# Column-group steps in a work list: the tiling switch counted in a step's length instead of in its earliest begin

## The chip, the cores and the metric

The kernel runs on one core of a Trainium2 chip. The core has a matrix engine (TensorE, in the profile PE, and PEld for its weight loads), a vector engine (VectorE, DVE), a scalar engine (ScalarE, ACT), a gather and scatter engine (GpSimd, POOL) and a queue engine that issues most transfers (SyncE, SP). Each engine works through its own instructions in the order in which the program lists them; semaphores make one wait for another. The metric is device time of one execution in microseconds, lower is better.

## The reference

Three layers follow one another on 2 x 768 tokens of 512 numbers: an attention with a window of 128 and four sink keys, a mixture of four attention experts, and a feed-forward mixture of eight experts in which each token goes to one expert. Only the third is touched here:

```python
def _moe2_ref(x, w_gate, w_local, w1, w2):        # w1 (8, 512, 1024), w2 (8, 1024, 512)
    ...
            p = np.exp(ls); p /= p.sum() + 1e-09
            h = np.maximum(x[b, s] @ w1[e], 0.0)
            out[b, s] = p[e] * (h @ w2[e])
```

The expert `e` of a token is found on the chip from `x @ w_gate` and a gate `x @ w_local`.

## The kernel before

The feed-forward layer (FFN) sorts the tokens by expert into **units** of 128 token rows. A unit gathers its rows (`unit_front`, `ga`, on POOL), transposes them (`tr`, line 1442), multiplies them with the expert's `w1` in two halves of 512 columns (`unit_first`, destination `hp`), applies ReLU (line 1502), transposes the result and multiplies it with `w2` (`unit_second`, destination `yp`), and scatters the rows to the output (`unit_end`, line 1540). A product of fp32 numbers is made of three matmuls of split operands (`mm3`, lines 306 to 308), so each weight tile of 256 x 512 is first split in two: `sp` copies it to the high part on ACT (line 1413) and subtracts on DVE (line 1421). A unit has eight such tiles (`raw` 83 to 90 in this build). `ld` loads them from HBM by SP (line 1397); a unit whose expert is that of the unit before it has its eight loads skipped on the chip by a condition, so that they are issued but move nothing. A unit is 24 matmuls of 512 columns for the first layer (six for each weight tile) and 24 for the second.

Experts with few tokens left over don't get a unit. Up to four such remainders of at most 32 rows (`PC` = 4, `PSZ` = 32) are computed together in `pieces()`: TensorE is switched to column groups of 32, and the four remainders stand side by side, each with its own expert's weights in plain fp32. This is cut in 16 **steps** (numbered 0 to 15, `s_` in the code): steps 0 to 3 and 4 to 7 are the two halves of the first layer, 8 to 15 the second layer. A step is a matmul for each of the four groups (line 1640; plain fp32 makes two passes of each, so the profile has eight instructions a step) and needs four weight tiles of 128 x 512, 256 KB each, which SP loads into a ring `qw` of 3 x 4 - 1 = 11 tiles (lines 1628 and 1630). From step 3 on a load is skipped on the chip where its group is empty. After steps 3 and 7 ACT applies ReLU (line 1646), TensorE transposes (line 1610) and ACT copies (line 1612); the last step's result goes through ACT (line 1651) to a scatter on POOL (line 1654).

The order of all this is set by a work list, not by hand. Each piece of work is a `Task` with an engine, an estimated length, the tasks it needs, ring slots it takes and frees, and a priority. `Order.run` keeps for each engine the time at which it becomes free by the estimates, asks `ready` for the earliest begin of each piece that can go, and gives out the one with the earliest begin; of equal ones the one with the lower priority number. The parts that matter:

```python
    def ready(self, t):
        e = self.free.get(t.eng, 0.0)
        if t.eng == "PE" and t.rows != self.rows:
            e += self.TURN                  # 0.093
        ...
                e, t = min(c, key=lambda x: (x[0], x[1].prio))
        ...
            if t.eng == "PE":
                self.rows = t.rows
```

`rows` marks work in another tiling of TensorE. Before the change a step has `rows=True`, the units' work has not. The steps' priority numbers are 200 and up by one hundred for each four steps, a unit's are about one hundred times its number. SP's loads are tasks of the same list, so where a step goes decides where its loads stand in SP's queue.

Static code reaches to unit 10; then each engine reads a register and branches (lines 1708 and 1718) on whether there is a further unit. With the given inputs there are twelve units, 0 to 11: 0 to 5 of one expert, 6 of a second, 7 to 11 of a third; three of the four groups of the steps hold rows.

Of the kernel before, what the change touches and what calls it, by code (L numbers as in the profile page):

```python
# [186 lines left out]
def d_a(n, extra=0):  # L187
    return (n / 1.2 + 52 + 93 * extra) / 1000
# [11 lines left out]
def fused_kernel(  # L200
# [858 lines left out]
    def at2(b, i, e=0.0):  # L1059
        return int(G * (b * NT + i + LAG + b * LAG1 + ESP * e / E1))  # L1060
# [181 lines left out]
    prev = None  # L1242
# [27 lines left out]
    for j0, n in groups:  # L1270
# [3 lines left out]
        prev = route(j0, n, at2(j1 // NT, j1 % NT, E1) + (RPO if j1 < T - 1 else 10), prev)  # L1274
# [161 lines left out]
    fo = order  # L1436
# [156 lines left out]
    def pieces():  # L1593

        at = 100 * QU
        def regs():
            R["np"] = nc.sync.value_load(eui[0:1, 2:3], min_val=0, max_val=PC)
            for p_ in range(PC):
                R["eq", p_] = nc.sync.value_load(eui[32 + p_:33 + p_, 0:1], min_val=0, max_val=E2 - 1)

        def ga():
            nc.gpsimd.indirect_dma_start(out=R["xg", "q"], out_offset=None, in_=x2d,
                                         in_offset=bass.IndirectOffsetOnAxis(ap=gixq, axis=0))
        g = fo.add("POOL", 1.4, ga, deps=[K["gixq"], K["ga", 1], K["eui"]], acq=[("xg", ("xg", "q"))], prio=at - 60)
        g = fo.add("GD", 0.8, lambda: None, deps=[g], prio=at - 60)

        def turned(key, src, dst, deps, pr, rel=()):
            def pe():
                for j in range(4):
                    nc.tensor.transpose(R[key][:, j * 128:(j + 1) * 128], src()[:, j * 128:(j + 1) * 128], ident)  # L1610
            a = fo.add("PE", 4 * D_TR, pe, deps=deps, acq=[("B", key)], prio=pr, rel=rel)
            return fo.add("ACT", d_a(512), lambda: nc.scalar.activation(dst, R[key], AF.Copy), deps=[a], prio=pr, rel=[key])
        ready = turned(("pq", "x"), lambda: R["xg", "q"], xq, [g, K["pu"]], at - 30, [("xg", "q")])
        prev = None
        for s_ in range(16):
            n, d = divmod(s_, 4)
            pr = at + 100 * (s_ // QN) + 16

            def wl(s_, p_, n=n, d=d):
                def f():  # L1620
                    if s_ == 0 and p_ == 0:
                        regs()
                    e = bass.ds(R["eq", p_], 1)
                    src = w1[e, d * 128:(d + 1) * 128, n * 512:(n + 1) * 512] if n < 2 else \
                        w2[e, (n - 2) * 512 + d * 128:(n - 2) * 512 + (d + 1) * 128, :]
                    src = src.rearrange("e p f -> p (e f)")
                    if s_ < 3:
                        nc.sync.dma_start(R["qw", s_, p_], src)
                    else:
                        nc.sync.dma_start(R["qw", s_, p_], src, cond=R["np"] > p_)  # L1630
                return f
            lds = [fo.add("DMA", 0.73, wl(s_, p_), deps=[K["eui"]], acq=[("qw", ("qw", s_, p_))], prio=at - 100 + 25 * s_ + p_)
                   for p_ in range(PC)]
            bank = ("hq", min(n, 2))

            def mm(s_=s_, n=n, d=d, bank=bank):
                src = xq if n < 2 else hTq[n - 2]
                for p_ in range(PC):
                    rows = slice(PSZ * p_, PSZ * (p_ + 1))
                    nc.tensor.matmul(R[bank][rows, :], src[:, d * 128 + PSZ * p_:d * 128 + PSZ * (p_ + 1)], R["qw", s_, p_],  # L1640
                                     start=s_ in (0, 4, 8), stop=s_ in (3, 7, 15))
            need = ready if n < 2 else K["hTq", n - 2]
            prev = fo.add("PE", 0.9, mm, deps=lds + [need] + ([prev] if prev else []), rows=True,
                          acq=[("B", bank)] if s_ in (0, 4, 8) else [], rel=[("qw", s_, p_) for p_ in range(PC)], prio=pr)
            if s_ in (3, 7):
                r_ = fo.add("ACT", d_a(512), lambda bank=bank: nc.scalar.activation(hq, R[bank], AF.Relu),
                            deps=[prev] + ([K["hTq", 0]] if n else []), rel=[bank], prio=pr + 1)
                K["hTq", n] = turned(("pq", n), lambda: hq, hTq[n], [r_], pr + 1)

        def ev():  # L1650
            nc.scalar.activation(R["yo", "q"], R["hq", 2], AF.Copy, scale=puq)

        def sc_():
            sct = nc.gpsimd.indirect_dma_start(out=out_rows, out_offset=bass.IndirectOffsetOnAxis(ap=sixq, axis=0),
                                               in_=R["yo", "q"], in_offset=None, bounds_check=T * C - 1, oob_is_err=False)
            for x in last_sc:
                tc.declare_no_dep(sct.ins, x.ins, reason="units hold disjoint rows")
            last_sc.append(sct)
        e_ = fo.add("ACT", d_a(512), ev, deps=[prev, K["puq"]], acq=[("yo", ("yo", "q"))], rel=[("hq", 2)], prio=pr + 10)
        f_ = fo.add("POOL", 1.1, sc_, deps=[e_], prio=pr + 10)  # L1660
        fo.add("GD", 0.0, lambda: None, deps=[f_], rel=[("yo", "q")], prio=pr + 10)
# [31 lines left out]
    for u in range(TS):  # L1693
        if u == 0:
            continue
        unit_front(u)
        if u == 1:
            sp(0, 3, 1, 10)
            unit_second(0, (1,))
            probabilities()  # L1700
            unit_end(0)
            pieces()
        unit_first(u)
        if u > 1:
            unit_second(u - 1)
# [58 lines left out]
```

## Time and profile before

| | |
|---|---|
| median of three runs | 453.91 us (452.2 to 455.86) |
| the profiled execution | 454.28 us, of which the traced span is 452.6 us |
| TensorE busy | 430.1 us, 95% of the span |
| VectorE busy | 351.9 us, 78% |
| ScalarE busy | 322.9 us, 71% |
| GpSimd busy | 146.4 us, 32% |

TensorE's busy time counts a matmul from its start to a modelled end, and a matmul that waits inside for its operand counts as busy, so stretches are better judged by the distance between starts. The FFN takes the span from about 255 us on.

### The profile page before, as it was taken

The numbers are of one execution on the slowest core, as the hardware profiler recorded it, in microseconds if no ns is written. First come the engines' busy times: TensorE is split into PE (matmuls) and PEld (weight loads), VectorE is DVE, ScalarE is ACT, GpSimd is POOL, SyncE is SP. The second block draws the span as 40 slices with busy tenths as digits, with TensorE's granted clock in tenths as the row PEclk, the third lists the DMA queues.
The fourth block names the chain that finished last, engine by engine and source line by source line (L and its number), as shares of the span: only waits on it lengthen the run. The fifth ranks groups of instructions, "written<-read, shape, count | busy, mean of one in ns | idle before, by whom it ended". The sixth has DMA issues, their size and how long they took to land.

```text
span 452.6 us, 10520 instructions
## 1 busy us (share of the span) xinstructions
PE 430.1 (95%) x3486; PEld 332.2 (73%) x3486; DVE 351.9 (78%) x1019; ACT 322.9 (71%) x759; POOL 146.4 (32%) x214
## 2 busy tenths in 40 slices
PE   8899999999999999999988999999999999968894
PEld 4579988779889778978866767678888888822283
DVE  2999696986997799698699879899998999810090
ACT  4799685966976898587387428899998989710180
POOL 8189912354030024200691142504671200000011
PEclk9999999999999999999999999999999999989999
DMA  7987241300300000000650228660697110069401
GB/s 163 175 182 189 66 101 46 71 25 18 79 25 1 25 3 25 25 3 25 224 174 25 70 84 274 203 216 18 210 375 275 45 48 23 25 199 299 153 29 52
DMA packets 58590, 48.28 MB, mean 107 GB/s; under 512 B 40863, under 2 KB 42399, under 8 KB 58528
## 3 DMA queue, kind: packets, MB, share of 16 engines
q1 hardware_dynamic: 56368, 40.72, 30.8%
q0 software_dynamic: 2160, 6.82, 4.3%
q8 instruction: 29, 0.48, 0.4%
q14 instruction: 33, 0.27, 0.2%
HBM read 86.58 MB, written 6.55 MB: 206 GB/s over the span
## 4 chain that ended last, share of the span: by engine, by line
PE 46%; issue 23%; DVE 17%; ACT 7%; DMA 3%; POOL 2%; POOLq 0%; SPq 0%; another core or an unknown queue 0%; ACTq 0%; DVEq 0%
PE bank L673 7%; PE bank L306 7%; PE bank L721 7%; PE bank L308 6%; PE bank L307 6%; PE bank L401 4%; DVE P L687 3%; DVE pT L728 3%; DMA raw<-in_moe_w_dram 2%; ACT P L697 2%; DVE wqk_l L1421 2%; PE bank L738 2%; PE bank L736 2%; POOL out_dram L1540 2%; PE bank L737 2%
## 5 line engine op out<-in xcount | busy, mean ns | idle before, releaser
L697 ACT ACTIVATE P<-P,nm 128x260 f32<-128x260 f32 (+4 forms) x160 | 84.0, 529 | 18.7 <-DVE nm L687 17.0
L1421 DVE TENSOR_TENSOR w<-raw,w 128x1024 fp32r<-128x1024 f32 x44 | 52.4, 1222 | 36.7 <-ACT w L1413 36.7
L728 DVE TENSOR_TENSOR pT<-bank,pT 128x512 f16<-128x512 f32 (+1 forms) x96 | 58.1, 629 | 13.3 <-ACT pT L724 12.8
L1540 POOL DMA_INDIRECT out_dram<-yof,six x12 | 31.8, 2653 | 68.0 <-ACT yof L1537 66.7
L724 ACT ACTIVATE pT<-bank 128x512 f16<-128x512 f32 (+1 forms) x96 | 49.1, 550 | 6.0 <-PE bank L721 4.9
L721 PE MATMUL bank<-ident,P 128*128 128x128 f32 x344 | 50.3, 278 | 0.9 <-ACT P L697 0.6
L1413 ACT ACTIVATE w<-raw 128x1024 fp32r<-128x1024 f32 x44 | 45.3, 1061 | 8.2 <-DMA x2d<-x 5.3
L687 DVE CUSTOM_DVE_ANT_0 P<-bank,mask 128x260 f32<-128x260 f32 (+1 forms) x96 | 36.5, 405 | 8.6 <-PE bank L673 8.5
L721 PEld LDWEIGHTS bank<-ident,P 128*128 128x128 f32 x344 | 38.2, 142 | 4.7 <-ACT P L697 2.6
L736 PEld LDWEIGHTS <-pT 128*128 128x128 f16 x344 | 30.8, 98 | 8.7 <-issue 2.6
L738 PEld LDWEIGHTS <-pT 128*128 128x128 f16 x344 | 30.6, 98 | 4.1 <-DVE pT L728 3.8
L673 PE MATMUL bank<-kT,qT 64*128 64x260 f32 (+1 forms) x192 | 31.6, 414 | 1.5 <-issue 1.1
L737 PEld LDWEIGHTS <-pT 128*128 128x128 f16 x344 | 31.0, 98 | 1.0 <-issue 0.3
L697 ACT ACTIVATION_READ_ACCUMULATOR P<-P,nm 128x1 f32 x160 | 31.2, 195 | 0.0
L401 PE MATMUL bank<-ident,raw 128*128 128x128 f32 x168 | 28.7, 292 | 0.5 <-POOL mask L331 0.2
L306 PE MATMUL bank<-xT,wqk_h 128*128 128x256 f32 x96 | 28.8, 299 | 0.0
L636 POOL TENSOR_SCALAR raw<-raw,s_sv 128x256 f32<-128x256 f32 x20 | 18.7, 945 | 28.1 <-DVE si_sv L532 17.6
L308 PE MATMUL bank<-xT,wqk_l 128*128 128x256 f32 x96 | 27.1, 282 | 0.0
L307 PE MATMUL bank<-xT,wqk_h 128*128 128x256 f32 x96 | 27.0, 281 | 0.0
L401 PEld LDWEIGHTS bank<-ident,raw 128*128 128x128 f32 x168 | 20.6, 164 | 7.8 <-DVE nm L687 1.7
L639 POOL CAST v<-raw 128x512 f16<-128x512 f32 x10 | 6.1, 610 | 59.4 <-PE bank L738 34.7
L687 DVE CUSTOM_DVE_ANT_0 P<-bank,cmask 128x384 f32<-128x384 f32 (+3 forms) x48 | 24.4, 528 | 1.0 <-PE bank L673 0.8
(432 smaller groups left out, 1332.4 us busy)
## 6 DMA issues: line engine op xcount, KB each, us to landing
raw<-in_moe_w_dram SPq DMA_DIRECT2D x104, 512.0 KB
qw<-in_moe_w_dram SPq DMA_DIRECT2D x64, 256.0 KB
raw<-in_v_dram SPq DMA_DIRECT2D x12, 256.0 KB
x2d<-x SPq DMA_DIRECT2D x12, 256.0 KB
raw<-in_q_dram SPq DMA_DIRECT2D x11, 256.0 KB
raw<-in_k_dram SPq DMA_DIRECT2D x11, 256.0 KB
raw<-in_moe_wv_dram SPq DMA_DIRECT2D x1, 512.0 KB
raw<-in_moe_wq_dram SPq DMA_DIRECT2D x1, 512.0 KB
```

What stands on the lines that cost most here:

```text
L306: nc.tensor.matmul(o, l[0], r[0], start=start, stop=False)
L307: nc.tensor.matmul(o, l[0], r[1], start=False, stop=False)
L308: nc.tensor.matmul(o, l[1], r[0], start=False, stop=stop)
L401: nc.tensor.transpose(p[:, j * 128:(j + 1) * 128], src(j), ident)
L673: nc.tensor.matmul(o, l, r, start=True, stop=True)
L687: nc.vector.tensor_tensor_reduce(p, s, sg["mask"], 0.0 if dead and st == 1 else -scale, gr["nm"] if si else 3.0e38, op0=OP.add, op1=OP.min ...
L697: nc.scalar.activation(p, p, AF.Exp, bias=gr["nm"], scale=-1.0, accum_out=sg["sum"]())
L721: nc.tensor.transpose(R[tk][:, j * 128:(j + 1) * 128], R[gr["P"]][:, c:c + 128], ident)
L724: nc.scalar.activation(R[sk_][0][:, :n * 128], R[tk][:, :n * 128], AF.Copy)
L728: nc.vector.tensor_sub(pl[:, :n * 128], R[tk][:, :n * 128], ph[:, :n * 128])
L1413: nc.scalar.activation(R["w", u, c, hf][0], R["raw", u, c, hf], AF.Copy)
L1421: eng.tensor_sub(wl[:, :, s_], R["raw", u, c, hf][:, :, s_], f32(wh)[:, :, s_])
```

## The change

The steps lose the mark `rows=True`, so `ready` adds nothing to the begin of a step, or to that of the piece behind it, and their length in the work list goes from 0.9 to 1.0.

```diff
@@ -1640,7 +1640,7 @@
             need = ready if n < 2 else K["hTq", n - 2]
-            prev = fo.add("PE", 0.9, mm, deps=lds + [need] + ([prev] if prev else []), rows=True,
+            prev = fo.add("PE", 1.0, mm, deps=lds + [need] + ([prev] if prev else []),
                           acq=[("B", bank)] if s_ in (0, 4, 8) else [], rel=[("qw", s_, p_) for p_ in range(PC)], prio=pr)
```

The matmuls are the same; their order isn't. The listings give an engine's instructions in a row, the line, the operation, what it writes and what it reads. `qw` are the steps' weight tiles, `ux` the transposed rows of a unit, `hT` those of its hidden layer, `wo`, `w_0`, `w_1`, `xT`, `wqk`, `wvg` slots that hold split weights.

On TensorE, in the first layer of unit 2, before the change:

```order
L307 MATMUL bank_80<-wo_l,ux_0_350 128x512
L308 MATMUL bank_80<-wo_h,ux_1_351 128x512
L306 MATMUL bank_80<-w_0_4402,ux_0_350 128x512
L307 MATMUL bank_80<-w_1_4403,ux_0_350 128x512
L308 MATMUL bank_80<-w_0_4402,ux_1_351 128x512
```

and after it, at the same place:

```order
L308 MATMUL bank_80<-wo_h,ux_1_351 128x512
L1442 MATMUL bank_82<-ident,hs_0_348 128x128 x4
L1640 MATMUL bank_77<-qw_0_4392,v2h_208 32x512
L1640 MATMUL bank_77<-qw_0_4393,v2h_208 32x512
L1640 MATMUL bank_77<-qw_0_4394,v2h_208 32x512
L1640 MATMUL bank_77<-qw_0_4395,v2h_208 32x512
L1640 MATMUL bank_76<-qw_0_4396,v2h_208 32x512
L1640 MATMUL bank_76<-qw_0_4397,v2h_208 32x512
L1640 MATMUL bank_76<-qw_0_4398,v2h_208 32x512
L1640 MATMUL bank_76<-qw_0_4391,v2h_208 32x512
L1610 MATMUL bank_79<-ident,v2l_209 128x128 x4
L306 MATMUL bank_80<-w_0_4402,ux_0_350 128x512
```

Steps 3 and 4 now stand between the third and the fourth weight tile of unit 2. In the whole listing steps 0 and 1 have moved ahead of the last twelve matmuls of unit 0, step 2 behind these, 5 to 7 ahead of and into unit 2's second layer, 8 to 10 around unit 3's second layer, 11 to 13 behind unit 4's first layer, 14 and 15 behind unit 5's; that makes twelve places. Before the change steps 0 and 1 and steps 2 and 3 were two places, and 4 to 15 a third.

On TensorE, at the end of the static code, before the change:

```order
L308 MATMUL bank_76<-wqk_h,hT_1_355 128x512
L1442 MATMUL bank_77<-ident,xgf_0_4412 128x128 x4
L1640 MATMUL bank_82<-qw_0_4396,v2h_208 32x512
L1640 MATMUL bank_82<-qw_0_4397,v2h_208 32x512
L1640 MATMUL bank_82<-qw_0_4398,v2h_208 32x512
```

and after it:

```order
L307 MATMUL bank_78<-w_1_4409,hT_0_354 128x512
L308 MATMUL bank_78<-w_0_4408,hT_1_355 128x512
L1442 MATMUL bank_82<-ident,xgf_0_4412 128x128 x4
L1708 TENSOR_LOAD eui
L1718 COMPARE_AND_BRANCH
```

The 48 matmuls of the twelve steps 4 to 15 that stood between the transposes of unit 11 and the branch are gone from there, with one set of four transposes among them.

On SP, whose loads the steps' waits reach, behind the third of unit 2's eight weight tiles, before the change:

```order
L1397 DMA raw_0_85<-in_moe_w_dram 128x2x512
L1397 ISA
L1397 REGISTER_ALU
L1397 ISA
L1397 DMA raw_0_86<-in_moe_w_dram 128x2x512
```

and after it, ahead of the fourth:

```order
L1630 ISA
L1630 DMA qw_0_4398<-in_moe_w_dram 128x512
L1630 ISA
L1630 DMA qw_0_4391<-in_moe_w_dram 128x512
L1397 ISA
L1397 REGISTER_ALU
L1397 ISA
L1397 DMA raw_0_86<-in_moe_w_dram 128x2x512
```

Nine loads of steps 2 to 4 now stand between the third and the fourth tile of unit 2; the last of them, into tile 4391, can be issued only when step 2 has read what is in it. In the same way loads of steps 5 to 8 stand ahead of unit 3's tiles and among them, 9 to 13 among those of units 3 to 5, and the last load of step 15 just ahead of unit 6's first. Before the change 37 of the 64 loads stood behind the tiles of unit 11.

## Rows read from the trace of the kernel before

**Rows 1.** Stretches of 10 us: busy time and count of each engine, clock, DMA.
```profile
core 0: us, PE busy (x) PEld busy (x) DVE busy (x) ACT busy (x) POOL busy (x), PEclk, DMA share, GB/s
...
290.00:300.00 10.00, 10.00 (x61) 7.07 (x60) 8.25 (x10) 7.60 (x12) 4.45 (x2) 1.00 0.67 217
300.00:310.00 10.00, 10.00 (x49) 8.19 (x49) 9.97 (x10) 10.00 (x14) 0.00 (x0) 1.00 0.50 159
310.00:320.00 10.00, 10.00 (x48) 8.14 (x47) 10.00 (x10) 10.00 (x13) 7.53 (x1) 1.00 0.02 7
320.00:330.00 10.00, 10.00 (x49) 8.22 (x48) 10.00 (x11) 10.00 (x13) 6.29 (x2) 1.00 0.84 288
330.00:340.00 10.00, 10.00 (x51) 8.19 (x50) 10.00 (x11) 9.02 (x13) 6.81 (x3) 1.00 1.04 391
340.00:350.00 10.00, 10.00 (x51) 8.23 (x50) 8.80 (x10) 8.68 (x13) 1.68 (x1) 1.00 0.76 288
...
400.00:410.00 10.00, 5.97 (x32) 1.61 (x28) 0.00 (x0) 1.19 (x2) 0.00 (x0) 0.83 0.94 296
410.00:420.00 10.00, 8.87 (x30) 1.53 (x28) 0.00 (x0) 0.00 (x0) 0.00 (x0) 1.00 0.91 296
420.00:430.00 10.00, 8.28 (x30) 2.54 (x29) 0.00 (x0) 1.68 (x3) 0.76 (x1) 1.00 0.39 133
```

**Rows 2.** TensorE in order of time: start us, length us, instruction, idle before and releaser.
```profile
397.03 0.60 PE L1442 MATMUL bank<-ident,xgf 128*128 128x128 f32 x4
397.56 2.78 PE L1640 MATMUL bank<-qw,v2h 128*32 128x512 f32 x24
403.65 3.06 PE L1640 MATMUL bank<-qw,v2h 128*32 128x512 f32 x8 [3.31 <-DMA qw<-in_moe_w_dram]
...
426.51 1.69 PE L1640 MATMUL bank<-qw,v2l 128*32 128x512 f32 x6 [1.71 <-DMA qw<-in_moe_w_dram]
428.13 0.50 PE L306 MATMUL bank<-w,uxf 128*128 128x512 f32 x1
```

**Rows 3.** DMA view of 397 to 428 us: packets, MB and share; issues, KB each.
```profile
q1 hardware_dynamic: 3888, 7.08, 70.3%
...
qw<-in_moe_w_dram SPq DMA_DIRECT2D x37, 256.0 KB
```

**Rows 4.** TensorE around steps 0 and 1, from unit 0's last twelve matmuls on.
```profile
284.36 0.39 PE L306 MATMUL bank<-xT,hT 128*128 128x512 f32 x1
...
286.89 0.40 PE L308 MATMUL bank<-wqk_h,hT 128*128 128x512 f32 x1
287.22 1.92 PE L1640 MATMUL bank<-qw,v2h 128*32 128x512 f32 x16
289.08 0.50 PE L306 MATMUL bank<-wqk_h,ux 128*128 128x512 f32 x1
289.42 0.39 PE L307 MATMUL bank<-wqk_l,ux 128*128 128x512 f32 x1
```

**Rows 5.** SP's queue in order of time, runs of loads of one line.
```profile
289.07 4.42 SPq L1630 DMA_DIRECT2D qw<-in_moe_w_dram  x7
...
398.77 23.45 SPq L1630 DMA_DIRECT2D qw<-in_moe_w_dram  x37
424.06 10.77 SPq L1397 DMA_DIRECT2D raw<-in_moe_w_dram  x8
```

**Rows 6.** Splits of unit 2's tiles from the fourth on, and TensorE's use of it.
```profile
289.10 3.48 DVE L1421 TENSOR_TENSOR w<-raw,w 128x1024 fp32r<-128x1024 f32 x3
...
288.40 2.00 ACT L1413 ACTIVATE w<-raw 128x1024 fp32r<-128x1024 f32 x2
...
293.37 0.40 PE L306 MATMUL bank<-w,ux 128*128 128x512 f32 x1
```

**Rows 7.** Unit 6: the first of its loads on SP, TensorE's first matmul.
```profile
320.18 1.53 SPq L1397 DMA_DIRECT2D raw<-in_moe_w_dram  x2
...
338.14 0.39 PE L306 MATMUL bank<-w,ux 128*128 128x512 f32 x1
```

## The prediction

> **What bounds the kernel now.** I read the stretches of 10 us first, then TensorE in order of time, then SP's queue. From 290 to 400 us TensorE is without a gap, and ACT and DVE, which split the weights, are close behind it: busy for 10.00 of 10 us in several stretches [rows 1]. At 397.56 us that ends. The twelve steps 4 to 15 stand there in one piece, and the next unit's matmul starts at 428.13 [rows 2], so the piece takes 30.57 us. In it DVE does nothing and ACT next to nothing, while the DMA engines are at 0.91 to 0.94 [rows 1]; TensorE stops with "DMA qw" as releaser [rows 2]. Of SP's loads for the steps 37 of 64 are issued only from 398.77 us on [rows 5], because the ring of 11 tiles was full until the first of these steps had run. 7.08 MB come in [rows 3], which is 27 tiles of 262,144 bytes: ten of the 37 are skipped, those of the empty group. So this piece is bound by its loads, and the rest of the FFN by TensorE, with the splits right behind. What follows the branch, 428.13 to the end, is units 10 and 11 on TensorE and isn't touched in amount.
>
> **The change, part by part.** Removed: the piece, 30.57 us.
>
> Added: the same matmuls among the units. Steps 0 and 1 start at 287.22 and the next matmul starts at 289.08, 1.86 us for two steps, 0.93 each [rows 4]; the three that run without a wait at 397.56 take 2.78 [rows 2], the same. Twelve steps are 11.16 us. The switch of tiling: matmuls of the units start every 0.23 us (eleven of them from 284.36 to 286.89 [rows 4]); the first step starts 0.33 behind the matmul before it, 0.10 more, and behind the steps the first matmul takes 0.34 to the next one, 0.11 more. That is 0.21 a place. The steps now stand in twelve places; two remain from before and the third went with the piece, so ten switches are added, 2.1 us. Four transposes go with the steps, 0.36 (0.53 from 397.03 to 397.56 [rows 2], less the switch and rounding). Together 13.6 us on TensorE, which is what sets the pace there. Without the switches it would be 11.5.
>
> Moved: 37 loads on SP, about 0.6 us each to issue (23.45 for 37 [rows 5]), of which 7.08 MB are data. They now go between 285 and 340 us. What was moved there before: 1.66 MB in 300 to 320, 9.67 MB in 320 to 350 [rows 1]. At the piece's 296 GB/s the first 20 us have room for 4.3 MB; at 391 GB/s, the most that a stretch shows, the next 30 have room for 2.1; the stretch itself gets 13.6 us longer, which is 4.0 more. 10.4 against 7.08: they fit, without much to spare.
>
> Added waits. SP now waits on TensorE at each of these loads (a tile must have been used), and the units' weight loads queue behind. I walk the narrowest places with the durations of the rows.
> (a) Step 2's last load can go when step 0 has used its tile, at about 285.5. A load of this kind lands after some 4.2 us: step 7's first is the second of the 37, issued at about 399.4, and TensorE goes on at 403.65 [rows 2, 5]. So 289.7, while TensorE arrives at 284.4 + 2.07 (steps 0, 1) + 2.8 (twelve matmuls) = 289.2: a wait of 0.5.
> (b) Unit 2's fourth tile is now issued behind step 2, which ends at 290.3: 0.3 and 0.6 for two issues, 1.5 until a skipped load counts as there (the load at 398.77 held back nothing at the end of the 2.78 us [rows 2, 5]), then ACT, held by a ReLU copy until 293.6, for 1.0, and DVE for 1.2 [rows 6]: 295.9. Before, the split was done at 290.3 and used at 293.37 [rows 6]. TensorE now gets there at 290.3 + 18 x 0.23 + 0.36 + 2.07 + 0.36 = 297.3. The lead falls from 3.1 to 1.4 us; no wait.
> (c) Step 5's loads are issued behind unit 2's tiles, the last at about 295.6, landed at 299.8; TensorE is there at 299.2: a wait of 0.6.
> (d) Unit 3's tiles follow loads that wait for step 5; in the same way of counting their splits are 0.2 to 1.9 us ahead of use. I put 0.4 for this place.
> (e) Later steps have their loads in 3 us or more before they stand.
> (f) Unit 6, whose weights are real loads, 4.2 MB, has its first issued behind the last of step 15, after step 13, at about 337 instead of 320.18; TensorE reaches unit 6 at 338.14 + 13.6 = 351.7 [rows 7]. It has 14.7 us instead of 18.0 for the first tile and 5.6 us of matmuls to receive the next three. No wait.
> Waits: 1.5 us; bounds 0 (all loads early enough) and 8 (two or three of these places late by one landing of 4.2 us). I take 1.5 because the walk is nearest to these rows.
> A landing of 4.2 us is measured under full DMA load, and the moved loads go out under less. The Trainium skill's "DMA: Bandwidth & Descriptors", section "Anatomy of one DMA", gives about 2.0 us plus the bytes at 436 GB/s, for a path that GpSimd issues. By that estimate a load would land after 2.6 us, (a) and (c) would not wait, and the sum would be 1.1 us lower.
>
> What the piece covered: ACT and DVE idled in it, POOL too; their work behind the branch (splits of unit 11's second layer) starts behind the branch in either kernel, and TensorE has some 12 us of other work before it needs them. Nothing at 0 but the branch itself: TensorE passes it without a gap before, 428.13 against the modelled end 428.20 [rows 2], with six matmuls of 1.69 us in hand. It now has six and four transposes, about as much. 0 us; if that cover failed, up to the 1.84 that SP needs from its last load at 422.22 to its first behind the branch [rows 5].
>
> Sum: -30.57 + 13.6 + 1.5 = -15.5. The profiled execution took 454.28, so 438.8; it was 0.37 above the median of the runs, so 438.4.
>
> **The rivals.**
> (1) The splits come late. If tiles of units 2 to 5 are held each time, ACT and DVE idle and TensorE waits for them. DVE is idle for 3.0 us of 290 to 350 [rows 1], and the longer stretch adds 13.6: 16.6. The walk has it idle about 4 us in each of (b) and (d), 8 in all. Should units 4 and 5 lose as much, the room is used up, and each further wait, or a bad order within a unit, is TensorE's: 4 to 11 us more, 442 to 450. For it: leads of 0.2 to 1.9 us, and ACT and DVE at 10.00. Against: the later loads lead by more.
> (2) The branch is exposed: 1.84 us more, 440.3. For it: no engine has idle time left ahead of it. Against: TensorE's missing gap. The Trainium skill's "Runtime: NRT & Kernel Launch", section "Instruction fetch mechanics", says that a taken branch breaks the sequential fetching and can stall until the target is there. The trace shows no such stall on TensorE, though behind a step that had just waited.
> (3) The wait moves along. TensorE waited 30.57 - 11.5 = 19.1 us in the piece for nine steps' loads. If the steps among the units still wait as long, because DMA serves them beside the units' weights, nothing is gained, 2.1 of switches are lost, and SP, held at each step, brings the weights of units 3 to 6 late by a landing of 4.2 us at one place or at all: 456 to 470. It decides from a mean wait of 1.3 us at each of the twelve steps (15.5 / 12) on. Against: between two steps lie 1.4 to 6 us of matmuls in which a load can land, and DMA was at 0.02 from 310 to 320 [rows 1].
> That the steps don't move can't be: the listing shows them moved.
>
> **How the numbers follow.** Forecast 0.68: from 434.8 (no waits, no switch cost: -30.57 + 11.5 = -19.1, less 0.37) to 442. (2) 0.05, inside it. (1) 0.18. (3) 0.09, of which 0.04 fall between 449.4 and 458.5. One per cent is 4.5 us, about what runs from 452.2 to 455.86 can tell from no change. Faster: 0.68 + 0.05 + 0.17 = 0.90; within 0.05; slower 0.05. The range reaches to 446, into (1): above it lie some 0.07 of (1) and the 0.09 of (3).
>
> **What would show it.** In the profile after, TensorE has no stretch with "DMA qw" as releaser of more than a microsecond or two; steps stand alone or in pairs between 284 and 350 us, about 0.93 us each; behind the transposes of unit 11, at some 412 us, the units' matmuls go on at once; unit 6's first matmul is near 352; DMA is busy from 300 to 320; the clock, granted at 0.83 in 400 to 410 [rows 1] (a mean of its two levels, 2.4 and 1.2 GHz, in a stretch that begins with 3.31 us of waiting [rows 2]), stays at 1.00. The prediction is wrong if DVE or ACT are named as releasers of units' matmuls for more than 3 us in sum between 290 and 350, if unit 6 waits for raw loads, or if the end behind the branch takes longer than its 24.5 us.

## The result, and the profile after

| | before | after |
|---|---|---|
| median | 454.88 us (4 runs) | 440.73 us (4 runs, 439.36 to 442.33) |
| ratio to before | | 0.9693, 95% interval 0.9629 to 0.9758 |
| profiled execution, span | 454.28 us, 452.6 us | 440.41 us, 438.6 us |

The change makes the kernel 3.1% faster: 14.15 us between the medians, 13.9 between the profiled executions. The forecast was 438.4.

To see where the time went, I measure both kernels from one mark to another: from the transposes of the remainders' rows (line 1610 on `xg`) to those of unit 11's rows (line 1442 on `xgf`), the last before the piece [rows 2]. TensorE before at the first mark:

```profile
282.47 0.66 PE L1610 MATMUL bank<-ident,xg 128*128 128x128 f32 x4
```

TensorE after, in order of time, from the first mark through the first half of the steps:

```profile
282.10 0.66 PE L1610 MATMUL bank<-ident,xg 128*128 128x128 f32 x4
...
284.08 1.92 PE L1640 MATMUL bank<-qw,v2h 128*32 128x512 f32 x16
285.93 0.50 PE L306 MATMUL bank<-xT,hT 128*128 128x512 f32 x1
...
288.90 1.06 PE L1640 MATMUL bank<-qw,v2h 128*32 128x512 f32 x8
289.90 0.50 PE L306 MATMUL bank<-wqk_h,ux 128*128 128x512 f32 x1
...
299.01 1.25 PE L1640 MATMUL bank<-qw,v2h 128*32 128x512 f32 x8
300.19 0.66 PE L1442 MATMUL bank<-ident,hs 128*128 128x128 f32 x4
...
306.17 1.72 PE L1640 MATMUL bank<-qw,v2h 128*32 128x512 f32 x8
307.82 0.50 PE L306 MATMUL bank<-w,hTf 128*128 128x512 f32 x1
```

The steps stand alone or in pairs, as foreseen. A pair takes 1.85 us, 284.08 to 285.93. A single step takes 1.00 (288.90 to 289.90). Two have waited inside: step 5 takes 1.18 and step 7 takes 1.65, so some 0.2 and 0.65 us of waiting.

From the last two steps to the branch:

```profile
342.83 1.92 PE L1640 MATMUL bank<-qw,v2l 128*32 128x512 f32 x16
344.68 0.50 PE L306 MATMUL bank<-wqk_h,hTf 128*128 128x512 f32 x1
...
352.38 0.40 PE L308 MATMUL bank<-w,hT 128*128 128x512 f32 x1
353.48 0.50 PE L306 MATMUL bank<-wo_h,ux 128*128 128x512 f32 x1 [0.70 <-ACT ux L1445]
...
354.87 0.50 PE L308 MATMUL bank<-wo_h,ux 128*128 128x512 f32 x1 [0.66 <-DVE ux L1449]
...
362.32 0.66 PE L1442 MATMUL bank<-ident,hs 128*128 128x128 f32 x4 [0.21 <-ACT hs L1502]
...
413.93 0.60 PE L1442 MATMUL bank<-ident,xgf 128*128 128x128 f32 x4
414.29 0.48 PE L306 MATMUL bank<-wo_h,hTf 128*128 128x512 f32 x1
```

The piece of 31.10 us behind the transposes of unit 11 (397.03 to 428.13 [rows 2]) is gone: behind the same transposes, at 413.93, the units go on after 0.36. From mark to mark it was 114.56 us and is 131.83, 17.27 more. With 0.37 less ahead of the first mark and 0.16 less behind the branch (24.47 and 24.31 us to the end of the span) that is 17.27 - 30.74 - 0.53 = -14.0, the difference of the spans. What was not foreseen stands in the middle: unit 6, whose first matmul stands at 353.48, waits for `ux`, the copy of its own rows.

Stretches of 10 us after (columns as in [rows 1]):

```profile
300.00:310.00 10.00, 10.00 (x54) 5.93 (x51) 5.34 (x7) 5.29 (x8) 1.01 (x1) 1.00 0.68 217
310.00:320.00 10.00, 10.00 (x55) 6.67 (x54) 9.47 (x10) 10.00 (x14) 1.29 (x1) 1.00 0.65 215
...
350.00:360.00 10.00, 8.64 (x36) 6.36 (x36) 9.44 (x11) 8.75 (x11) 4.47 (x3) 1.00 1.05 389
400.00:410.00 10.00, 10.00 (x48) 8.18 (x46) 8.95 (x9) 8.98 (x12) 0.98 (x1) 1.00 0.07 28
```

DMA now works where it was idle (0.65 against 0.02 in 310 to 320 [rows 1]); ACT and DVE lose work time early (5.3 us of 10 in 300 to 310), and TensorE doesn't notice, since no split is named as releaser there. The clock is granted at 1.00 in 400 to 410, where it was 0.83 around the waits.

### The profile page after: what moved, and what is told of

Its sections match the earlier page's. It is cut to its first block, busy times and chain, and to the rows that moved or that the text cites. A ratio compares the mean times of both kernels' runs of the same rounds, so it can differ in the third digit from the quotient of the medians.

```text
span 438.6 us, 10515 instructions
## 1 busy us (share of the span) xinstructions
PE 420.7 (96%) x3486; PEld 329.7 (75%) x3486; DVE 352.2 (80%) x1019; ACT 323.1 (74%) x759; POOL 129.9 (30%) x214
## 4 chain that ended last, share of the span: by engine, by line
PE 56%; DVE 16%; issue 16%; ACT 6%; DMA 3%; POOL 2%; SPq 1%; POOLq 0%; another core or an unknown queue 0%; ACTq 0%; DVEq 0%
PE bank L306 9%; PE bank L308 9%; PE bank L307 8%; PE bank L721 7%; PE bank L673 6%; DVE P L687 4%; PE bank L401 3%; DVE pT L728 3%; PE bank L1640 3%; DMA xg<-x2d,gix 2%; PE bank L738 2%; PE bank L736 2%; ACT P L697 2%; PE bank L1442 2%; PE bank L737 2%
## 5 line engine op out<-in xcount | busy, mean ns | idle before, releaser
L728 DVE TENSOR_TENSOR pT<-bank,pT 128x512 f16<-128x512 f32 (+1 forms) x96 | 58.0, 627 | 13.6 <-ACT pT L724 13.1
L1540 POOL DMA_INDIRECT out_dram<-yof,six x12 | 13.8, 1150 | 67.5 <-ACT yof L1537 66.3
L1462 POOL DMA_INDIRECT xgf<-x2d,gix x9 | 11.2, 1246 | 62.1 <-PE bank L1442 56.6
L1421 DVE TENSOR_TENSOR xT<-raw,xT 128x1024 fp32r<-128x1024 f32 x17 | 20.6, 1216 | 6.9 <-ACT xT L1413 6.8
```

What stands on the lines that cost most here:

```text
L728: nc.vector.tensor_sub(pl[:, :n * 128], R[tk][:, :n * 128], ph[:, :n * 128])
L1421: eng.tensor_sub(wl[:, :, s_], R["raw", u, c, hf][:, :, s_], f32(wh)[:, :, s_])
```

## The experiments

The theory: the mark puts steps 4 to 15 in one piece that nothing covers; it is bound by its loads; spread out, the steps cost their matmuls and switches, and what came on top is one split on ACT that waits for unit 6's weights and holds the copy behind it. Against it stand, one by one, that the length did it, that SP's issuing or the data rate bound the piece, and that the moved loads cost more among the units than the waits show. Each ratio below is to runs of the kernel before that were made beside it (medians 454.3 to 455.7 us).

### Which part of the change does it

e1_length_only: before, with the length alone. e2_mark_only: after, with the length put back.

```diff
-  prev = fo.add("PE", 0.9, mm, deps=..., rows=True,     # e1, against before
+  prev = fo.add("PE", 1.0, mm, deps=..., rows=True,
-  prev = fo.add("PE", 1.0, mm, deps=...,                # e2, against after
+  prev = fo.add("PE", 0.9, mm, deps=...,
```

> Only the length of a step in the work list goes from 0.9 to 1.0; the steps keep their mark, so that the switch still counts in when they can begin. The theory (it is where the steps stand that costs, and the mark sets it): steps 4 to 15 stay in one piece behind the transposes of unit 11, some 31 us, and the time is that of the kernel before, 454 to 456 us. The rival (the length does it): the steps spread and the time is 439 to 442 us.

> Only the mark is taken away, the length stays at 0.9. The theory: without the mark the steps spread among the units, in fourteen places instead of twelve, most of them single, so that two more switches at about 0.2 us are added; 440 to 442 us, no piece in front of the branch. The rival (length and mark are needed together, since the order that the longer step gives is the good one): some steps pile up again or waits of several us appear, 445 us and more.

Measured: e1 453.85 us, ratio 0.9952 (0.9928 to 0.9976); the piece stands from 400.63 to 430.74, 30.1 us. e2 442.13 us, ratio 0.9714 (0.9689 to 0.9739), its steps in fourteen places; the intervals don't tell it from the change. So the mark holds the steps back and taking it away moves them. What the length adds to that e2 can't tell from nothing; that e1, with the length alone, is half a per cent faster than before isn't traced.

### What bounded the piece

Four kernels change what the piece has to load: e3 skips the loads from step 3 on, e8 skips none, e10 has a smaller ring, e12 that ring and no loads for the empty group.

```diff
-  nc.sync.dma_start(R["qw", s_, p_], src, cond=R["np"] > p_)        # e3
+  nc.sync.dma_start(R["qw", s_, p_], src, cond=R["np"] > p_ + PC)
-  if s_ < 3:                                                        # e8: all without condition
+  if s_ < 16:
-  bufs["qw"] = ring(ff, 3 * PC - 1, ...)                            # e10 and e12
+  bufs["qw"] = ring(ff, 9, ...)
-  lds = [... for p_ in range(PC)]                                   # e12 as well
+  lds = [... for p_ in range(PC - 1)]
-  nc.tensor.matmul(..., R["qw", s_, p_],
+  nc.tensor.matmul(..., R["qw", s_, min(p_, PC - 2)],
```

> The kernel before, with every load of the steps' weights from step 3 on skipped on the chip (issued, but nothing moves), so that these steps multiply with stale weights. It tells what the piece of 31 us was bound by. The theory (the 7.08 MB that came in there): the twelve steps, no longer fed by anything, take 11.5 to 14 us from the first to the next unit's matmul, and the time is 436 to 439 us. The rival (SP's issue, 37 loads at 0.63 us each, 23.4 us): the piece stays at 23 to 27 us and the time at 447 to 452 us.

> The kernel before, with no load of the steps' weights skipped: those of the empty group are moved too, so ten more of the 37 in the piece, 2.6 MB. The theory (bound by the data): at the 296 GB/s of the piece they take 8.9 us more, and the time is 461 to 465 us. The rival (bound by SP's issue): the piece stays at 31 us, the time within 1 us of before, or up to 3 us below, since a load without a condition is issued faster.

> The kernel before, with a ring of 9 tiles for the steps' weights instead of 11; steps 4 to 15 stay in one piece. In the runs without data the piece took 12.2 us, and with ten tiles more it took 32.3 instead of 30.6, at 391 GB/s instead of 296; so it isn't the rate of 296 GB/s that bounds it. The theory now (the round trip: a tile is freed, its load is issued, lands and is used, and only 11 tiles are on the way): the piece grows as 11 to 9, to about 37 us, and the time to 460 to 462 us. The rival (the rate that the memory gives to these loads): the piece stays at 30 to 32 us, the time at 454 to 456 us.

> The kernel before, with a ring of 9 tiles and with no loads at all for the fourth group of the steps, which is empty for these inputs; its matmuls read the third group's weights instead, and its rows go nowhere. Steps 3 to 15 stand in front of the branch, and 30 loads stand there, all of which move data; in the run with 9 tiles and four groups 39 stood there, 29 of which moved data, and the piece took 32.1 us. The theory (a load that is skipped holds up the loads behind it nearly as long as one that moves data, so what counts is the number of loads, 0.63 to 0.68 us each): the piece is 25 to 28 us and the time 448 to 451 us. The rival (what counts is the data): the same data or a little more, 32 to 33 us, and 455 to 457 us.

TensorE of e3 in the piece:

```profile
396.21 3.64 PE L1640 MATMUL bank<-qw,v2h 128*32 128x512 f32 x32
400.64 0.66 PE L1610 MATMUL bank<-ident,v2l 128*128 128x128 f32 x4 [0.80 <-ACT v2l L1646]
401.23 3.64 PE L1640 MATMUL bank<-qw,v2h 128*32 128x512 f32 x32
404.69 3.76 PE L1640 MATMUL bank<-qw,v2l 128*32 128x512 f32 x32
408.37 0.50 PE L306 MATMUL bank<-w,uxf 128*128 128x512 f32 x1
```

SP's loads in the piece, of e3, e8, e10 and e12, one fence each:

```profile
397.41 9.96 SPq L1630 DMA_DIRECT2D qw<-in_moe_w_dram  x37
```

```profile
397.98 25.09 SPq L1628 DMA_DIRECT2D qw<-in_moe_w_dram  x37
```

```profile
398.15 25.95 SPq L1630 DMA_DIRECT2D qw<-in_moe_w_dram  x39
```

```profile
398.94 23.22 SPq L1630 DMA_DIRECT2D qw<-in_moe_w_dram  x30
```

| kernel | loads in the piece that move data | that are skipped | steps | piece, us | time, us | ratio |
|---|---|---|---|---|---|---|
| before [rows 2, 3, 5] | 27 | 10 | 12 | 30.57 | 454.9 | |
| e3 | 0 | 37 | 12 | 12.16 | 435.89 | 0.9599 (0.9562 to 0.9636) |
| e8 | 37 | 0 | 12 | 32.26 | 456.94 | 1.0046 (1.0015 to 1.0077) |
| e10 | 29 | 10 | 12 | 32.10 | 456.10 | 1.0038 (1.0011 to 1.0065) |
| e12 | 30 | 0 | 13 | 29.64 | 453.30 | 0.9962 (0.9927 to 0.9996) |

e3 settles the first question: without their data the same twelve steps take 12.16 us, 0.80 of them a wait for a ReLU. The piece was bound by its loads; the matmuls didn't hold it. It does not tell the data from SP's issuing, because a skipped load costs SP less as well: SP issues the 37 in 9.96 us where the kernel before takes 23.45 [rows 5]. So e3 did not test its rival.

How the loads bound it is less simple, and three expectations fell. It isn't a rate of 296 GB/s: with ten tiles more (e8) the piece grows by 1.7 us, not 8.9, and DMA moves 388 GB/s in 410 to 420. It isn't the round trip of a full ring: with 9 tiles (e10) it grows by 1.5, no more than two more loads with data would make it (30.57 x 29 / 27 = 32.8), not to 37. It isn't the mere count either: 30 loads, all with data (e12), take 29.64, neither the 25 to 28 of the one theory nor the 32 to 33 of the other. What it is in the kernel before, SP's own row shows. SP before, in 409.6 to 422.2 us:

```profile
409.67 12.55 SPq L1630 DMA_DIRECT2D qw<-in_moe_w_dram  x21
```

There SP waits for nothing that the trace shows, and issues the four loads of a step in 2.5 us: 0.67 to 0.73 us for each of the three that move data under a condition, 0.42 for the skipped one. That is 0.786 MB in 2.5 us, 315 GB/s, and each of these loads has landed 3.1 to 3.9 us after its issue, but for the last two (5.7). So SP's issuing set the pace there, as the rival of e3 had it, but the issuing of loads that move data. In e8 a load, which has no condition, takes SP 0.53 us. SP's waits there in 411.8 to 422.2 us, and the stretch from 410 us:

```profile
SPq L1628 <- PE bank L1640: 2.3, 4, 0.6
```

```profile
410.00:420.00 10.00, 10.00 (x31) 2.06 (x30) 0.00 (x0) 0.00 (x0) 0.00 (x0) 1.00 1.05 388
```

SP has time left, and a load lands every 0.68 us, at 388 GB/s, near the 391 that is the most in [rows 1]: there the data set the pace. A DMA share of 0.91, as in the kernel before [rows 1], still left room; here it is 1.05. In e10 and e12 SP takes 0.72 us for a load with data, 0.43 for a skipped one, and waits for freed tiles besides, once for 1.6 us in e12. No run makes issuing cheaper and leaves the data as it is, so how much shorter the piece would be with that isn't shown; the explanation of the change doesn't need it.

### What the steps and unit 6 still wait for

e4 is the changed kernel with unit 6's weight loads skipped, e7 the one with the steps' loads skipped, e6 has an estimate that differs.

```diff
-  nc.sync.dma_start(raw, src, cond=R["e", u] != R["e", u - 1])      # e4
+  nc.sync.dma_start(raw, src, cond=R["e", u] > R["e", u - 1])
-  K["ld", u, c, hf] = add("DMA", CLD if u > 1 else 1.46, f, ...)    # e6; CLD is 0.4
+  K["ld", u, c, hf] = add("DMA", (2.0 if u == 6 else CLD) if u > 1 else 1.46, f, ...)
-  nc.sync.dma_start(R["qw", s_, p_], src, cond=R["np"] > p_)        # e7
+  nc.sync.dma_start(R["qw", s_, p_], src, cond=R["np"] > p_ + PC)
```

> The changed kernel, with the loads of unit 6's weights skipped on the chip, so that unit 6 multiplies with the weights of unit 5. The theory (the first real load comes 2.9 us after ACT is free for it, ACT works in order, and the copy of unit 6's rows stands behind six splits): TensorE's waits at unit 6, 1.1 us in all behind the 0.23 us rhythm at the first matmul, 0.8 at the third and 0.4 at the transposes, go, and the time is 438 to 439 us, about 2 us below the changed kernel. The rival (the copy is late because ACT is full of work there anyway): it stays within 1 us of the changed kernel, and the waits on ux stay.

> The changed kernel, with unit 6's loads estimated at 2.0 us instead of 0.4 in the work list. TensorE's and SP's order stay the same (some banks change names late); on ACT and VectorE the copy of unit 6's rows moves ahead of two splits. The theory (the order on ACT makes the wait): the copy is done 1.9 us earlier, unit 6's first matmul follows without a wait, and the time is 438.5 to 439.5 us, 1 to 2 us below the changed kernel. The rival (the load itself is what comes late, whatever the order): the wait moves to the splits of unit 6, 440 to 441 us.

> The changed kernel, with the loads of the steps' weights from step 3 on skipped on the chip, so that these steps multiply with stale weights. The theory (the steps cost their matmuls and switches, 14.1 us, and behind their data only the waits at steps 5 and 7 and at unit 6, some 3 us in all): 437.5 to 439 us. The rival (the 7 MB beside the units' own loads cost more than the waits show, in slower splits or loads): 434 to 437 us, the time that the kernel before takes without them.

Measured: e4 438.09 us, ratio 0.9639 (0.9578 to 0.9701); e6 438.46, 0.9656 (0.9590 to 0.9723); e7 438.60, 0.9660 (0.9593 to 0.9728). The intervals overlap with that of the change, so the marks in the traces must tell it. SP of the changed kernel, then ACT in order of time:

```profile
334.70 2.61 SPq L1630 DMA_DIRECT2D qw<-in_moe_w_dram  x5
339.14 60.21 SPq L1397 DMA_DIRECT2D raw<-in_moe_w_dram  x44
```

```profile
340.39 0.59 ACT L1502 ACTIVATE hs<-bank 128x512 f32<-128x512 f32 x1
343.87 1.06 ACT L1413 ACTIVATE wo_h<-raw 128x1024 fp32r<-128x1024 f32 x1 [2.89 <-DMA raw<-in_moe_w_dram]
345.18 1.06 ACT L1413 ACTIVATE w<-raw 128x1024 fp32r<-128x1024 f32 x1 [0.26 <-DMA raw<-in_moe_w_dram]
...
347.10 2.07 ACT L1413 ACTIVATE w<-raw 128x1024 fp32r<-128x1024 f32 x2
349.07 0.67 ACT L1651 ACTIVATE yof<-bank,puq 128x512 f32<-128x512 f32 x1
349.64 2.24 ACT L1413 ACTIVATE wqk_h<-raw 128x1024 fp32r<-128x1024 f32 x2
...
352.83 0.60 ACT L1445 ACTIVATE ux<-bank 128x512 fp32r<-128x512 f32 x1
```

Unit 6's first tile is issued at 339.14, behind the last load of step 15. ACT is free at 340.98 (the copy at 340.39 and its 0.59) and starts the tile's split at 343.87, after 2.89 us of waiting. The copy of unit 6's rows stands behind six such splits and comes at 352.83, though the transposes that it copies are from 349.40. ACT of e6, where that copy is two splits further ahead and the orders of TensorE and SP are unchanged:

```profile
343.82 1.06 ACT L1413 ACTIVATE wo_h<-raw 128x1024 fp32r<-128x1024 f32 x1 [3.54 <-DMA raw<-in_moe_w_dram]
...
350.20 0.62 ACT L1445 ACTIVATE ux<-bank 128x512 fp32r<-128x512 f32 x1
350.68 2.04 ACT L1413 ACTIVATE wqk_h<-raw 128x1024 fp32r<-128x1024 f32 x2
```

and its TensorE at unit 6:

```profile
351.68 0.40 PE L308 MATMUL bank<-w,hT 128*128 128x512 f32 x1
351.92 0.39 PE L306 MATMUL bank<-wo_h,ux 128*128 128x512 f32 x1
```

The tile comes as late as before (ACT waits 3.54 us for it), and TensorE doesn't wait at all. So TensorE paid for the late load only through its place in ACT's row, ahead of the copy. In e4 there is no such wait on ACT, and in e7 SP is free for unit 6 earlier:

```profile
336.64 7.84 SPq L1397 DMA_DIRECT2D raw<-in_moe_w_dram  x9
```

From step 14 to the second mark the changed kernel takes 71.10 us (342.83 to 413.93), and e4, e6 and e7 take 68.75 each: 341.55 to 410.30, 342.13 to 410.88, 342.46 to 411.21. The wait of unit 6 is worth 2.35 us.

e7 gives the rest as well. Its TensorE at the first mark, step 14 and the second mark:

```profile
282.57 0.66 PE L1610 MATMUL bank<-ident,xg 128*128 128x128 f32 x4
...
342.46 1.92 PE L1640 MATMUL bank<-qw,v2l 128*32 128x512 f32 x16
...
411.21 0.60 PE L1442 MATMUL bank<-ident,xgf 128*128 128x128 f32 x4
```

From the first mark to step 14 it takes 59.89 us (282.57 to 342.46) and the changed kernel 60.73: the steps' waits for their data are 0.84. That is one execution; e6 and e4, whose loads are the same up to there, have 0.17 and 1.23 (60.06 and 61.12 us). And from mark to mark e7 takes 128.64, against 114.56 before: the steps without any wait add 14.08.

### How near the edge the moved loads are

e9_after_all_step_loads: the change of e8, made to the changed kernel.

> The changed kernel, with no load of the steps' weights skipped: thirteen tiles more, 3.4 MB, among the units. It tells how near the moved loads are to the point at which the wait moves along. The theory (there is room for some 3 MB more, worked out as 10.4 against 7.08 MB): the waits at steps 5 and 7 grow by a us or two each and unit 6's weights come as late as before, 441 to 445 us. The rival (the loads are on the edge, each tile more is a wait of its own): each of the twelve steps waits for a us or more, and the time is 450 us or above.

Measured: 444.84 us, ratio 0.9794 (0.9754 to 0.9834). TensorE at steps 3 to 5 and at unit 6:

```profile
294.82 3.24 PE L1640 MATMUL bank<-qw,v2h 128*32 128x512 f32 x16
298.00 0.65 PE L1610 MATMUL bank<-ident,v2l 128*128 128x128 f32 x4
...
300.43 1.60 PE L1640 MATMUL bank<-qw,v2h 128*32 128x512 f32 x6
303.23 1.04 PE L1640 MATMUL bank<-qw,v2h 128*32 128x512 f32 x2 [1.20 <-DMA qw<-in_moe_w_dram]
...
357.40 0.50 PE L306 MATMUL bank<-wo_h,ux 128*128 128x512 f32 x1 [1.21 <-ACT ux L1445]
```

Steps 3 and 4 now take 3.18 us instead of 1.86, and step 5 takes 3.77 instead of 1.18; steps 6 to 15 don't wait (1.06 or 1.07 us long where single, 1.92 in a pair), step 7 among them, for which a longer wait was expected. Unit 6 waits 1.21 us for `ux` instead of 0.70. So the tight places are the first ones, and 3.4 MB more cost 4.1 us between the medians, 3.6 from mark to mark (135.40 against 131.83). The wait doesn't move along. The loads here have no condition, so each also takes SP less time, as in e8.

### Other places for the steps

e5 lets the steps begin at unit 7, where no unit has weights to load; e11 also gives out two steps as one piece of work, in eight places.

```diff
-QU = 2                                     # e5 and e11
+QU = 7
+  if s_ % 2 == 0:                          # e11, mm as before
+      kept, mm0 = lds, mm
+      continue
-  prev = fo.add("PE", 1.0, mm, deps=lds + ...
+  prev = fo.add("PE", 1.95, two, deps=kept + lds + ...     # two() is mm0(), then mm()
```

> The changed kernel, with the steps' turn put at unit 7, so that they stand among units 7 to 10, where no unit has weights to load. The theory (what was not foreseen are waits behind loads that unit 6's real loads and the steps share; each of ten places of steps costs 0.2 us wherever it is): unit 6 no longer waits, the steps have their loads in time, and the time is 437 to 439 us. The rival (the steps' own loads hold SP and ACT wherever they stand): waits of 2 us or more at the steps or at the splits of units 7 to 10, 440 to 443 us; and the last step may still wait near the branch.

> The changed kernel with the steps' turn at unit 7, and two steps given out as one piece of work, so that there are eight places of two steps instead of twelve, eight of them single. The theory (a place costs its two switches of tiling, 0.21 us, and a single step 0.06 more): four places and eight singles fewer, 1.3 us, so 437 to 437.7 us where the steps' turn alone gave 438.7. The rival (a pair needs eight tiles of the ring at once, so its loads come later, and the last pair stands right in front of the branch): waits of 1 us or more at several pairs, 439 to 442 us.

Measured: e5 438.67 us, ratio 0.9643 (0.9574 to 0.9713); e11 437.64, ratio 0.9627 (0.9595 to 0.9659). In neither does a step wait; both wait for a ReLU copy between 291 and 292 us, for 0.83 and 0.84 us, e5 for a second one for 0.53, and e11 once for its rows for 0.23. TensorE of e11 at the last pair:

```profile
409.25 1.92 PE L1640 MATMUL bank<-qw,v2l 128*32 128x512 f32 x16
411.10 0.50 PE L306 MATMUL bank<-wqk_h,uxf 128*128 128x512 f32 x1
```

The pair takes 1.85 and its loads hold nothing up. e11 is the fastest kernel here by its median, 3.1 us below the changed one, though the intervals of the two ratios still overlap; that pairs are worth 1.0 us against e5 agrees with the 1.3 worked out, but the runs can't tell it from nothing.

## Why the prediction was right, and where it was off

**The piece.** Right. Its 30.57 us went (30.74 between the marks), because the steps' loads were what it waited for, as e3 shows. That the 296 GB/s of the stretch was a rate to reckon with was wrong: e8 moves 388, and in the kernel before it was SP's issuing, four loads in 2.5 us, that kept it lower. The rate only served to show that the loads fit, which they did: DMA at 0.62 to 0.77 in 290 to 340.

**What the steps add.** 13.6 predicted, 14.08 measured without waits. The 0.5 is the price of a single step: 0.99 to 1.00 to the next start where half a pair's 1.86 is 0.93, and there are eight of them.

**The waits.** 1.5 predicted, 0.84 at the steps and 2.35 at unit 6 measured. (a) No wait at step 2, where 0.5 was put: 288.90 to 289.90. (c) 0.2 at step 5, where 0.6 was put. (b) and (d): the splits of units 2 and 3 hold TensorE nowhere, so rival (1) did not come. (e) was wrong for step 7, which waits 0.65. (f), "No wait" at unit 6, is the step that failed. Its times were near: first tile issued at 339.14 instead of 337, TensorE ready at 352.6 instead of 351.7. But it asked only when tiles come and TensorE needs them. It did not count that the first split holds up all that ACT has in its row behind it, the copy of the unit's own rows among it. e6 shows this as the cause, by another order with the same load.

Of the 1.5 us only 0.2 came where it was put. That the sum of the waits was off by no more than 1.7 us is luck as much as reckoning.

The prediction had named "if unit 6 waits for raw loads" as a sign of being wrong. It came by way of ACT, which waits 2.89 and 0.26 us for `raw`, and TensorE behind it for the copies. The other signs stayed away: between 290 and 350 us neither DVE nor ACT is named as what a unit's matmul waited for, and the end behind the branch takes 24.3 us.

A landing of 4.2 us, from a busy stretch, was the value for (a) and (c). The estimate from the Trainium skill's "DMA: Bandwidth & Descriptors", section "Anatomy of one DMA", 2.6 us for a path that GpSimd issues, had both without a wait. For the 512 KB tile of unit 6 the same formula gives an estimate of 3.2 us, and the trace shows 4.73 from issue to the start of the split. By the completion events in the trace (a load's semaphore at its full count) neither 4.2 nor 2.6 holds everywhere. At (a) the last load was issued at 285.15 us and had landed after 2.99, ahead of TensorE at 288.90. At (c) the last one with data, issued at 295.64, had landed after 3.52, and TensorE stood there from 299.01 on. Step 7's, issued at 301.20, took 5.60, and TensorE came at 306.17: this is what (e) missed, for 4.2 would have been in time.

**The branch.** Right at 0: 0.36 us from the transposes to the next matmul, which is their own length. The Trainium skill's "Runtime: NRT & Kernel Launch", section "Instruction fetch mechanics", says that a taken branch can stall; no run here shows that on TensorE.

**Rival (3).** The steps don't wait 1.3 us each but 0.07 in the mean (0.84 / 12). e9 shows the margin: with 3.4 MB more, waits come at the first places alone.

**The sum.** By the terms measured: -30.74 + 14.08 + 0.84 + 2.35 = -13.5, with 0.53 of small differences outside the marks -14.0; predicted -15.5.

## What to carry to other kernels

A task list that charges a switch of mode to when a piece of work can begin never gives that work out while other work is ready, and here that put 7 MB of loads and the matmuls behind them at the end of the list, where nothing covered them; charge it to the length, or leave it out, which made no difference that could be measured here (e2). When loads are queued on one engine, look at that engine's row too: in the piece it was SP's time to issue them, not what the DMA engines can move, that set the pace. When loads are moved, follow each engine's row, not only the tile: the first instruction that waits for a late load also holds up short copies behind it that have nothing to do with that load. Such a wait may go by reordering the row (e6), with the load as late as it was.

## What the runs showed of the hardware

Loads of 256 KB came in at 293 to 296 GB/s with skipped ones among them (before, e10), at 323 with none skipped (e12) and at 388 with no condition on them (e8), in 410 to 420 us each. SP takes about 0.7 us to issue one under a condition (0.67 to 0.73 in the kernel before, 0.72 in e10 and e12), 0.53 for one without (e8), 0.42 for a skipped one among loads with data (before) and 0.23 to 0.28 where all are skipped (e3). Loads of 256 KB had landed 2.6 to 5.7 us after their issue (the kernel before and the changed one). A single column-group step costs 0.06 us more than half a pair, beside its two switches.
